# Attention and two MLPs on one core: fp32 scores from q and k turned by TensorE, W1o loaded into buffers of its own, and another loop order in one product

## The chip, the cores and the metric

The kernel runs on one core of a Trainium2 chip. The metric is the device time of one execution in microseconds (us). Engines: PE is TensorE, DVE is VectorE, ACT is ScalarE, POOL is GpSimd, SP is SyncE, which here only issues DMAs. Each engine works through its own instructions in the order in which they are written.

## What is computed

Attention with rotary positions over 4 batches, 8 heads, 576 positions and 64 dimensions; its output, 2304 tokens of 512, goes through two MLPs, 512 to 2048 to 512 each.

```python
q_rot, k_rot = rotate(q), rotate(k)          # x1*cos - x2*sin, x1*sin + x2*cos
scores = (1 / sqrt(D)) * q_rot @ k_rot.T
attn = exp(scores - scores.max(-1)); attn = attn / (attn.sum(-1) + 1e-9)
x = (attn @ v)                               # B, H, S, D -> tokens x 512
h = x @ moe_w_in;  x = (h * sigmoid(1.702 * h)) @ moe_w_out
h = x @ moe2_w_in; out = where(h > 0, h, exp(min(h, 0)) - 1) @ moe2_w_out
```

All tensors are fp32.

## The kernel before

**Numbers.** Nearly every product runs in f16: an operand is scaled by a power of two and split into a high half and a low half, and a product is the sum of three (high x high, high x low, low x high; `THIRD`). Splitting costs one instruction for the high half (ACT or DVE) and one for the low half (DVE) for each tile.

**Order.** A class `Plan` takes operations with their inputs, buffers and a key (constants in `TUNE`) and writes each engine's order out before anything runs. Buffers of a name are few (`BUFS`): two score tiles `s` in PSUM, three general PSUM tiles `m`, two tiles `E` of exponentials. A change of keys or buffers writes all engines' orders anew.

**Attention.** `prep(b, hp)` prepares q and k of one batch and a pair of heads (16 in all): largest magnitude (ACT, L600), its way across the partitions by PE and DVE (L350, L354, L357, L360), the scale (L606 to L612), the rotation (DVE, L618, L622, L626), high halves (ACT, L632, L638), low halves (DVE, L641) and one DMA transpose into `qkT` (L653). `s_unit` is one head against 128 query positions: four f16 products of 288 columns into a score tile `s` (L753), the maximum (DVE, L757) and its product with the scale (L761), the exponential with its sum (ACT, L765), reciprocal (L772, L776), high and low halves (L781, L783, L787) and a DMA transpose into `et` (L796). The last 64 positions of both heads make a "tail" unit of eight products. `av_unit` multiplies with v (L822, L825, L829).

**First MLP.** Tokens go in blocks: 128, 256 and 192 in batch 0, 320 and 256 in the others. `first_mlp` makes first products with W1i (L872; 12 for each of 16 slices), a tanh form of the activation (ACT L875, DVE L878), the halves of g in `ghl` (L887, L890), and second products with W1o (L909), evicted at L915. The first products of a block are written to wait for the second products of the block before (`prev`). W1i and W1o are loaded raw into four buffers `G`, which are the memory of `ghl`: so all W1i loads stand on SP's queue ahead of W1o's, and block 0's halves of g wait for the whole of W1o to be read out (`W1o.raw_done`). `class Weight` finds each matrix's scale (L420 to L453) and splits it (ACT L496, DVE L498 and L502; for W1i's first 12 tiles PE makes the low half, L510 and L511).

**Second MLP.** Five blocks of 512 tokens, the last of 256. First products with W2i (L1104), ELU (ACT L1107, DVE L1111, L1115), halves (L1079, L1082, L1087), then the product with W2o. For block 0 that is L1235: for each of four token tiles, 16 slices of 128 rows, three products each, 192 products of 512 columns. The other blocks use seven quarter-size products on sums of operands (L1180); the sums of W2o's quarters are made behind block 0 (`weight_sums`, DVE L977, ACT L994).

The order of block 0's last product:

```python
for tt in range(n // P):            # 4 token tiles
    for c in range(4):              # 4 chunks of 4 slices of W2o
        ...                         # 12 products, L1235, into the tile's "m" bank
```

Of the kernel before, what the change touches and what calls it, by code (L numbers as in the profile page):

```python
# [20 lines left out]
    s=2, av=1, m=3, E=2, Ehl=3, et=2, qkT=3, N16=1, R=1, V=4, T=1, v16=3, x=9, t=3, y=1, R2=3, yhl=1, o=3,  # L21
)
TUNE = dict(
    pe_w1i=12, pe_w1o=0, lsame=218.42826132665004, tab=-77.15647150906182, f_dve=397.65103425170275, f_act=47.97551796307805, f_pool=12.224437399728332,
    w2s=460.6613102590577, w1i2=-22.170419296187163, w1o2=-231.93668493230768, dlat=823.3988909607715, qh=36.14175031675045,
    kt=-88.54498457451459, vam=-5.163260596687561, p0=0, lat=344.9241913205742, slack=1000000000.0, w1i=-77.58934967679743,
    w1i_s=6.138443343881177, w1o=93.92320162730282, w1o_s=0.9525910530680881, prep0_s=2.7543259438533925, nt=5.6622832505119804,
    s_f=40.3256386921686, mx_f=6.7540349396707375, ex_f=7.075547533776429, av_f=14.806376760777082, prep0=18.144612418330304,
    prep=-131.80876126536305, va0=-49.3683499402336, va=-205.2411204142313, vs=0.522839907570051, tiny=5.266502586522658,
    av=-64.29097871435411, ex=-84.71729381432783, mx=0.5562209547683765, s=-2.701464647252074, tr=-84.32125296728447,  # L30
    bits=-53.84333624001694,
# [190 lines left out]
def kernel(  # L222
# [32 lines left out]
    for b in range(B):  # L255
        parts = ([([0], False), ([1, 2], False), ([3], True)], [([0, 1], True), ([2, 3], False)], [([0, 1], False), ([2, 3], True)])[TUNE['p0'] if b == 0 else 1]
# [52 lines left out]
    buf("qkT", ap_, [P, 6, 5 * P], F16, BUFS["qkT"])  # L309
    n16 = ap_.tile([P, 6, 5, P], F16, name="n16")  # L310
    buf("N16", lambda i: n16, None, None, 1)
    buf("R", ap_, [P, 1280], F32, BUFS["R"])
    buf("V", ap_, [P, 640], F32, BUFS["V"])
    buf("T", ap_, [P, 4, 5, D], F32, BUFS["T"])
# [24 lines left out]
    def across(am, n, hM, after, key, add=False, use=()):  # L339
# [3 lines left out]
        if add:  # L343
            def total(e):
                nc.tensor.matmul(take(hM)[:, 256:256 + n], square, am(), start=True, stop=True)
# [15 lines left out]

        o = op({"pe": 300.0}, turn, list(after) + [ready_c], key, need=[("m", hM)], use=use)
        o = op({"dve": 220.0 + 220.0 * (n > 1)}, most, [o], key, use=[hM], port=n > 1)
        return op({"pe": 200.0}, back, [o, lit], key, use=[hM])

    def max_scale(am, name, bufs, after, key, add=False, mul=1.0):
# [10 lines left out]
        o = across(am, 1, hM, after, key, add)  # L377
# [170 lines left out]
    tab = ap_.tile([P, 10, D], F32, name="tab")  # L548
# [5 lines left out]
    am_t = [per.tile([P, 2], F32, name=f"am{i}") for i in range(2)]  # L554
    ghl = per.tile([P, 2, KF, NMAX], F16, name="ghl")
    gh, gl = ghl[:, 0], ghl[:, 1]
    gflat = ghl.rearrange("p t a b -> p (t a b)")
    buf("G", lambda i: (gh, gl)[i // 2].rearrange("p a b -> p (a b)").bitcast(F32)[:, 1024 * (i % 2):1024 * (i % 2) + 1024], None, None, 4)

    def start(e):  # L560
        nc.sync.dma_start(out=eye, in_=tab_d[:, 10:12, :].rearrange("p a d -> p (a d)"))
        nc.sync.dma_start(out=tab, in_=tab_d[:, 0:10, :])

    def light(e):
        nc.gpsimd.memset(n16[:, 4:6, :, D:2 * D], 0.0)
# [11 lines left out]
    csc = {}  # L577
    am_last = {}

    def prep(b, hp):  # L580
        key = first_u[fb[b], hp] - TUNE["prep"] if b else first_u[0, hp] * TUNE["prep0_s"] - TUNE["prep0"]
        h0 = 2 * hp
        st = {}
        hR, hT, hN, hX, hG = [(x, b, hp) for x in ("R", "T", "N16", "qkT", "qkg")]

        def R5():
            return take(hR).rearrange("p (t h j d) -> p t h j d", t=2, h=2, j=5)

        def load(e):
            R = R5()  # L590
            nc.gpsimd.memset(take(hR).rearrange("p (a f) -> p a f", a=4)[64:P, :, 256:320], 0.0)
            for t, src in enumerate((q, k)):
                nc.sync.dma_start(out=R[:, t, :, 0:4, :], in_=src[b, h0:h0 + 2, 0:512, :].rearrange("h (p j) d -> p h j d", j=4))
                nc.sync.dma_start(out=R[0:64, t, :, 4, :], in_=src[b, h0:h0 + 2, 512:S, :].rearrange("h p d -> p h d"))

        def amax(e):
            am = am_t[hp % 2]
            if e == "act":
                for t in range(2):
# [733 lines left out]
```

## Time and profile before

| | us |
|---|---|
| device time, median of 3 runs | 1068.86 (1068.05 to 1069.65) |
| span of the profiled execution | 1067.2 |
| PE busy | 956.5 (90%) |
| DVE busy | 910.9 (85%) |
| ACT busy | 664.0 (62%) |

The span runs from the first to the last instruction of one profiled execution on the core. A table of stretches gives each engine's busy time, the granted clock of PE and the share of the DMA engines for a part of the span; a timeline gives one engine's instructions with start and duration, neighbours of one kind joined (x12 is twelve instructions), and in brackets the idle time ahead of them with what ended it. Since neighbouring products overlap in the pipeline, a price is read from one row's start to the next one's.

### The profile page before, as it was taken

To read this page: it belongs to the slowest core of one execution; us is meant where nothing else is said; L and a number is where in the kernel's file an instruction comes from. 1 tells how busy PE (TensorE), PEld (TensorE's weight loads), DVE (VectorE), ACT (ScalarE), POOL (GpSimd) and SP (SyncE) were. 2 spreads that over 40 slices of the span, in tenths; PEclk is the share of its full clock that TensorE was granted. 3 is DMA by queue.
4 is the path that set the end of the run, shared out by engine and by line. 5 is a ranking of instruction groups with operands and counts; after the bars stand their busy time and mean duration, and the time that the engine had idled before them with its cause. 6 is when DMAs were issued, how large, how long until landed. Compare 5 with 4: busy or idle time off the path is not lost. (4 is left out here: it accounts for less than half of the span.)

```text
span 1067.2 us, 20467 instructions
## 1 busy us (share of the span) xinstructions
PE 956.5 (90%) x7710; PEld 682.2 (64%) x7710; DVE 910.9 (85%) x2075; ACT 664.0 (62%) x1233; POOL 6.8 (1%) x25
## 2 busy tenths in 40 slices
PE   1457658999989999999999999996999999999997
PEld 0223437877876678876788778642445855855886
DVE  7899999998989999999895979899969669569474
ACT  5688889785868788787563738565246136146141
POOL 0000000000000000000000000000000000000000
PEclk9987669999999999999999999997999999999999
DMA  8899967597878797877754434600000200200100
GB/s 275 242 219 223 232 147 126 123 166 169 165 156 158 141 199 146 159 141 147 168 113 159 156 109 121 212 22 1 21 20 1 65 15 1 65 15 2 45 16 20
DMA packets 295010, 124.94 MB, mean 117 GB/s; under 512 B 264960, under 2 KB 284032, under 8 KB 294912
## 3 DMA queue, kind: packets, MB, share of 16 engines
q1 hardware_dynamic: 294912, 123.64, 50.4%
q8 instruction: 60, 0.98, 0.4%
q14 instruction: 38, 0.31, 0.1%
HBM read 53.35 MB, written 9.44 MB: 59 GB/s over the span
## 5 line engine op out<-in xcount | busy, mean ns | idle before, releaser
L872 PE MATMUL m<-x,wi 128*128 128x256 f16 (+3 forms) x1728 | 199.4, 273 | 1.2 <-DVE t L878 1.1
L909 PE MATMUL m<-ghl,wo 128*128 128x256 f16 (+3 forms) x1728 | 198.7, 273 | 0.3 <-ACT y L915 0.2
L1104 PE MATMUL m<-yhl,w2i 128*128 128x512 f16 (+1 forms) x960 | 188.3, 358 | 0.5 <-DVE e L1115 0.3
L872 PEld LDWEIGHTS <-wi 128*128 128x128 f16 x1728 | 156.7, 98 | 36.1 <-issue 5.5
L909 PEld LDWEIGHTS <-wo 128*128 128x128 f16 x1728 | 157.4, 98 | 33.7 <-issue 3.3
L1104 PEld LDWEIGHTS <-w2i 128*128 128x128 f16 x960 | 93.9, 98 | 92.9 <-issue 1.0
L765 ACT ACTIVATE E<-s,st,qk_c 128x576 f32<-128x576 f32 x144 | 118.7, 826 | 25.4 <-DVE st L761 13.6
L787 DVE SCALAR_TENSOR_TENSOR Ehl<-E,st,Ehl 128x576 f16<-128x576 f32 x144 | 116.6, 813 | 7.4 <-ACT Ehl L781 7.0
L753 PE MATMUL s<-qkT 128*128 128x288 f16 (+1 forms) x640 | 99.6, 302 | 24.4 <-ACT E L765 24.2
L757 DVE TENSOR_REDUCE st<-s 128x1 f32<-128x576 f32 x144 | 107.0, 751 | 7.7 <-PE s L753 7.2
L781 ACT ACTIVATE Ehl<-E,st 128x576 f16<-128x576 f32 x119 | 91.1, 771 | 30.0 <-DMA et<-Ehl 19.6
L1107 ACT ACTIVATE e<-m,y_c 128x512 f32<-128x512 f32 (+1 forms) x80 | 50.8, 639 | 78.0 <-issue 47.9
L753 PEld LDWEIGHTS <-qkT 128*128 128x128 f16 (+1 forms) x640 | 56.5, 104 | 49.8 <-issue 35.9
L1180 PEld LDWEIGHTS <-g 128*128 128x128 f16 x714 | 70.4, 99 | 9.5 <-issue 0.7
L1200 DVE SCALAR_TENSOR_TENSOR x<-z,eo,x 128x256 f32<-128x256 f32 x49 | 23.4, 482 | 50.3 <-PE z L1180 50.0
L875 ACT ACTIVATE t<-m,hsc 128x320 f32<-128x320 f32 (+3 forms) x96 | 55.2, 575 | 14.5 <-PE m L872 12.8
L822 PE MATMUL av<-et,v 128*64 128x256 f16 (+3 forms) x720 | 54.4, 301 | 9.5 <-DMA et<-Ehl 9.3
L887 ACT ACTIVATE ghl<-t 128x320 f16<-128x320 f32 (+3 forms) x96 | 49.9, 521 | 17.9 <-DVE t L878 17.2
L1180 PE MATMUL z<-wo,g 128*128 128x256 f16 x504 | 58.0, 277 | 0.0
L1235 PE MATMUL m<-w2o,g 128*128 128x512 f16 x192 | 50.0, 413 | 8.5 <-DVE w2o L502 5.9
L878 DVE SCALAR_TENSOR_TENSOR t<-t,m 128x320 f32<-128x320 f32 (+3 forms) x96 | 52.7, 551 | 4.2 <-ACT t L875 3.8
L890 DVE SCALAR_TENSOR_TENSOR ghl<-t,ghl 128x320 f16<-128x320 f32 (+3 forms) x96 | 53.1, 554 | 3.4 <-ACT ghl L887 3.2
(172 smaller groups left out, 1389.4 us busy)
## 6 DMA issues: line engine op xcount, KB each, us to landing
ghl<-in_moe_w_in_dram SPq DMA_DIRECT2D x16, 512.0 KB, 5.1
ghl<-in_moe_w_out_dram SPq DMA_DIRECT2D x16, 512.0 KB, 4.7
R<-in_moe_w_in_dram SPq DMA_DIRECT2D x16, 512.0 KB, 4.2
R<-in_moe_w_out_dram SPq DMA_DIRECT2D x16, 512.0 KB, 3.8
R<-in_q_dram SPq DMA_DIRECT2D x16, 256.0 KB, 2.9
R<-in_k_dram SPq DMA_DIRECT2D x16, 256.0 KB, 3.2
V<-in_v_dram SPq DMA_DIRECT2D x32, 128.0 KB, 3.0
R<-y_d SPq DMA_DIRECT2D x8, 512.0 KB, 3.9
```

The lines of the kernel that those rows point to most:

```text
L753: nc.tensor.matmul(o, X[:, a, t], X[:, 2 + 2 * x + a, cs], start=x == 0, stop=x == 1)
L757: nc.vector.tensor_reduce(out=st["t"][:, 0:1], in_=take(hS)[:, :, 0:NS], axis=AX.XY, op=ALU.max, negate=True)
L765: nc.scalar.activation(out=take(hE).rearrange("p (c f) -> p c f", c=2), in_=take(hS)[:, :, 0:NS], func=AF.Exp, bias=t[:, 1:2], scale=csc[b ...
L781: nc.scalar.activation(out=X16[:, 0:S], in_=take(hE), func=AF.Copy, scale=st["t"][:, 3:4])
L787: nc.vector.scalar_tensor_tensor(out=X16[:, S:2 * S], in0=E, scalar=r, in1=X16[:, 0:S], op0=ALU.mult, op1=ALU.subtract)
L822: nc.tensor.matmul(ps[64 * a:64 * a + 64, 0:N], W[:, j, a, :] if w == 2 else V[:, w, j, a, :], T[:, a, blk, 0:N], start=i == 0, stop=i == ...
L872: nc.tensor.matmul(ps, W1i.lhs(kk, u, wl), x[:, xl, 0:N], start=kk == 0 and i == 0, stop=kk == KD - 1 and i == 2)
L875: nc.scalar.activation(out=flat(ht), in_=flat(hM), func=AF.Tanh, scale=hsc[b][:, 1:2])
L890: nc.vector.scalar_tensor_tensor(out=g_of(gl), in0=t_of(), scalar=DOWN / 2, in1=g_of(gh), op0=ALU.mult, op1=ALU.subtract)
L909: nc.tensor.matmul(ps[:, 0:N], W1o.lhs(f, d, wl), (gh, gl)[xl][:, f, 0:N], start=f == 0 and i == 0, stop=f == KF - 1 and i == 2)
L1104: nc.tensor.matmul(ps[:, 0:n], W2i.lhs(kk, u, wl), Y[:, xl, kk, 0:n], start=kk == 0 and i == 0, stop=kk == KD - 1 and i == 2)
L1180: nc.tensor.matmul(ps, AT[A](p, gi, P * tt), BT[B](p, wl), start=p == 0 and i == 0, stop=p == 7 and i == 2)
```

## The change

**Scores in fp32.** Scales, halves and the DMA transpose of q and k are gone. `prep` now rotates q and k (the factor 1/sqrt(D) stands in the table of cosines for q) into a tile `T` that holds both heads side by side, PE turns it in nine transposes of 128x128 (three groups of three, L595), and ACT moves each group of 384 columns into an fp32 `qkT` (L600). `s_units` is both heads of 128 positions at once: four fp32 products of 288 columns, head 0 on rows 0 to 63 and head 1 on rows 64 to 127, into both `s` tiles (L702). Maximum (L707), exponential (L711), halves (L727, L729, L733) and transposes stay one for each head; sum and reciprocal (L718, L722) serve both. In the tail the two heads take the two halves of the keys in opposite order. There are three `E` and two `T` buffers, two `qkT` instead of three.

**W1o and the first blocks.** Raw W1o loads into two buffers of its own (`Go`), and block 0's halves of g no longer wait for it. Batch 0's blocks are 128, 192 and 256 tokens; first products of blocks 0 and 1 (L821) wait for no second product (L858), and block 1's g stands beside block 0's in `ghl`.

**The last product of block 0** in the second MLP (L1180) runs chunk by chunk, all four token tiles within a chunk, on four PSUM banks `z`.

The keys in `TUNE` are others, so all orders are new.

```diff
@@ BUFS
-    s=2, av=1, m=3, E=2, Ehl=3, et=2, qkT=3, N16=1, R=1, V=4, T=1, v16=3, x=9, t=3, y=1, R2=3, yhl=1, o=3,
+    s=2, av=1, m=3, E=3, Ehl=3, et=2, qkT=2, R=1, V=4, T=2, v16=3, x=9, t=3, y=1, R2=3, yhl=1, o=3,
@@ prep
...
+        def turn(e, g):
+            ps = take(hX + (g,))
+            for s in range(3):
+                nc.tensor.transpose(ps[:, P * s:P * s + P], take(hT)[:, 3 * g + s].rearrange("p h d -> p (h d)"), eye)
+
+        def put(e, g):
+            X, ps = take(hX)[:, 3 * P * g:3 * P * g + 3 * P], take(hX + (g,))[:, 0:3 * P]
...
+                nc.scalar.activation(out=X, in_=ps, func=AF.Copy)
...
-        am = op({"act": 2 * c_act(640, acc=1), "dve": c_dve(1280)}, amax, [ld, am_last.get(hp % 2)], key, use=[hR])
-        rd = am_last[hp % 2] = across(lambda: am_t[hp % 2], 2, hG, [am], key)
-        sc = op({"dve": 560}, scale, [rd], key, use=[hG], port=True)
...
-        kh = op({"act": c_act(1280, ptr=1)}, k_hi, [r3, sc], key, need=[("N16", hN)], use=[hR])
-        qh = op({"act": c_act(640, ptr=1)}, q_hi, [kh], key, use=[hR, hN])
-        kl = op({"dve": c_dve(640, ptr=1)}, k_lo, [kh], key, use=[hR, hN], port=True)
-        ql = op({"dve": c_dve(640, ptr=1)}, q_lo, [qh], key, use=[hR, hN], port=True)
-        t = op({"dma": 5200.0}, 2300.0, tr, [ql, kl], key - TUNE["kt"], need=[("qkT", hX)], use=[hN])
...
@@ s_unit, now s_units
         def mm(e):
-            X, ps = take(hX), take(hS)
+            X = take(hX)
             for c in range(2):
-                cs = slice(c * NS, c * NS + NS)
-                for x in range(2):
-                    for a in range(2) if h is None else [h]:
-                        o, t = (ps[64 * a:64 * a + 64, c, 0:NS], slice(512, S)) if h is None else (ps[:, c, 0:NS], slice(j * P, j * P + P))
-                        nc.tensor.matmul(o, X[:, a, t], X[:, 2 + 2 * x + a, cs], start=x == 0, stop=x == 1)
...
+                for a in range(2):
+                    r = slice(64 * a, 64 * a + 64)
+                    if h is None:
+                        w = (c + a) % 2
+                        o, t = take(hS[0])[r, w, 0:NS], S
+                    else:
+                        w = c
+                        o, t = take(hS[a])[:, c, 0:NS], S + 64 + P * j
+                    nc.tensor.matmul(o, X[r, t:t + (TAIL if h is None else P)], X[r, NS * w:NS * w + NS], start=True, stop=True)
...
@@ first_mlp
-                deps = [x_ready[n, kk] for kk in range(KD)] + W1i.slice_ready(v + w) + [prev]
+                deps = [x_ready[n, kk] for kk in range(KD)] + W1i.slice_ready(v + w) + [before]
...
-            o = op({"act": c_act(W * N)}, hi, [o] + (W1o.raw_done if n == 0 else []), -9e4, use=[ht])
+            o = op({"act": c_act(W * N)}, hi, [o], -9e4, use=[ht])
...
-        prev = first_mlp(n, prev, h_ok, y_ok)
+        prev = first_mlp(n, prev if n > 1 else None, prev, h_ok, y_ok)
@@ second_mlp, last product of block 0
-            for tt in range(n // P):
...
-                for c in range(4):
...
+            for c in range(4):
+                for tt in range(n // P):
...
+                    o = op({"pe": c_mm(512, 12)}, lambda e, tt=tt, c=c: mm(e, tt, c), gr[4 * c:4 * c + 4] + W2o.ready[4 * c:4 * c + 4] + prev_out[-1:], kp + 18 + 4 * c + tt, need=[] if c else [("z", hM)], use=[hM] if c else [])
```

On SP, raw W1o loads stood behind all W1i loads; they now stand among the first of these.

PE's order at a score unit, before, while W1i's low halves are made (`eye`, `am0` and `diag2` belong to the turn of the maxima, `wi` to the weights, `s1` is a score tile):

```order
L350 MATMUL m1_480<-eye_75,am0_80 2x128
L510 MATMUL m0_488<-wi_97,w1i_eye_352 128x512
L511 LDWEIGHTS minus_76
L511 MATMUL m0_488<-wi_97,minus_76 128x512
L360 MATMUL m1_480<-diag2_151,square_78 128x2
L753 LDWEIGHTS qkT0_302
L753 MATMUL s1_498<-qkT0_302 128x288
```

And now, among second products of block 0, nine transposes of one `T` and one unit of two heads:

```order
L595 MATMUL m1_1681<-eye_74,T0_1262 128x128 x3
L595 MATMUL m0_1693<-eye_74,T0_1262 128x128 x3
L595 MATMUL m2_1703<-eye_74,T0_1262 128x128 x3
L702 MATMUL s0_1710<-qkT1_1064 128x288
L702 MATMUL s1_1712<-qkT1_1064 128x288
L702 MATMUL s0_1710<-qkT1_1064 128x288
L702 MATMUL s1_1712<-qkT1_1064 128x288
L858 LDWEIGHTS wo_200
L858 MATMUL m1_1723<-ghl_79,wo_200 128x128
```

The turn of the maxima is gone, the transposes have come, and scores of two heads alternate.

PE's order at the place where block 0's second products begin, before (`x` is the attention's output, `wi` and `wo` the weights, `ghl` the halves of g):

```order
L872 MATMUL m0_1766<-x7_1450,wi_97 128x128
L872 LDWEIGHTS wi_97
L872 MATMUL m0_1766<-x7_1450,wi_97 128x128
L909 LDWEIGHTS wo_396
L909 MATMUL m2_1838<-ghl_82,wo_396 128x128
```

And now, where first products of block 1 (192 columns) stand among second products of block 0:

```order
L858 LDWEIGHTS wo_200
L858 MATMUL m1_1723<-ghl_79,wo_200 128x128
L821 LDWEIGHTS wi_93
L821 MATMUL m0_1739<-x1_648,wi_93 128x192
L821 LDWEIGHTS wi_93
```

First products of block 1 no longer stand behind the second products of block 0.

DVE's order at the end of the sums of W2o's quarters, before (`R20` holds a sum, `e0` is a tile of the next block's ELU, `w2o` the weight):

```order
L977 TENSOR_TENSOR R20_9748<-w2o_7745,R20_9748 128x256
L977 TENSOR_TENSOR R20_9748<-R20_9748,w2o_7745 128x256
L977 TENSOR_TENSOR wo_396<-R20_9748,wo_396 128x1024
L1111 TENSOR_SCALAR e0_9854<-e0_9854 128x512
L1115 SCALAR_TENSOR_TENSOR e0_9854<-m2_9825,y_c_8634,e0_9854 128x512
L1082 SCALAR_TENSOR_TENSOR ghl_82<-e0_9854,y_c_8634,ghl_82 128x256
```

And now at the same place:

```order
L926 TENSOR_TENSOR R20_9195<-w2o_7127,R20_9195 128x256
L926 TENSOR_TENSOR R20_9195<-R20_9195,w2o_7127 128x256
L1060 TENSOR_SCALAR e0_9232<-e0_9232 128x512
L1064 SCALAR_TENSOR_TENSOR e0_9232<-m1_9200,y_c_8016,e0_9232 128x512
L926 TENSOR_TENSOR wo_200<-R20_9195,wo_200 128x1024
L1060 TENSOR_SCALAR e1_9254<-e1_9254 128x512
L1031 SCALAR_TENSOR_TENSOR ghl_79<-e0_9232,y_c_8016,ghl_79 128x256
```

The first ELU of the next block stands one instruction earlier, behind 71 of the 72 rows of sums.

## Rows read from the trace of the kernel before

**Rows 1.** The page, busy time of each engine: us (share of the span) xinstructions.

```profile
PE 956.5 (90%) x7710; PEld 682.2 (64%) x7710; DVE 910.9 (85%) x2075; ACT 664.0 (62%) x1233; POOL 6.8 (1%) x25
```

**Rows 2.** Stretches: bounds, us, busy PE, PEld, DVE, ACT, POOL, clock, DMA share, GB/s.

```profile
0.00:189.00 189.00, 104.51 (x913) 67.75 (x914) 172.85 (x410) 149.34 (x283) 3.75 (x15) 0.83 0.88 209
189.00:570.00 381.00, 371.63 (x3557) 296.30 (x3555) 345.00 (x872) 284.83 (x568) 3.07 (x10) 1.00 0.75 152
...
725.00:750.00 25.00, 16.48 (x44) 4.69 (x42) 24.38 (x43) 11.26 (x17) 0.00 (x0) 0.63 0.00 0
...
785.00:1022.00 237.00, 236.60 (x1611) 156.96 (x1610) 175.85 (x359) 95.05 (x140) 0.00 (x0) 1.00 0.09 25
```

**Rows 3.** PE's timeline, 156 to 191 us: start, duration, operation, [idle before].

```profile
158.67 2.17 PE L872 MATMUL m<-x,wi 128*128 128x128 f16 x36
...
188.53 2.64 PE L909 MATMUL m<-ghl,wo 128*128 128x128 f16 x40
```

**Rows 4.** DVE's timeline, 182 to 187 us.

```profile
185.22 0.75 DVE L502 SCALAR_TENSOR_TENSOR wo<-wo,w1o_s 128x512 f16<-128x512 f32 x1
185.88 0.15 DVE L772 TENSOR_SCALAR st<-st 128x1 f32<-128x1 f32 x1
```

**Rows 5.** DVE's groups by form: count | us in all, mean ns of one | idle before.

```profile
L641 DVE SCALAR_TENSOR_TENSOR n<-R,qk_s,n 128x640 f16<-128x640 f32 x32 | 27.9, 877 | 0.6 <-ACT n L632 0.4
...
L761 DVE TENSOR_TENSOR st<-st,qk_c 128x1 f32<-128x1 f32 x144 | 21.3, 152 | 0.3
```

**Rows 6.** PE's waits, 0 to 205 us: us in all, times, longest us.

```profile
PE s L753 <- ACT E L765: 17.9, 16, 3.1
```

**Rows 7.** PE's timeline, 380 to 400 us.

```profile
382.42 0.66 PE L753 MATMUL s<-qkT 128*128 128x288 f16 x4
382.92 1.79 PE L909 MATMUL m<-ghl,wo 128*128 128x320 f16 x12
...
386.77 0.68 PE L753 MATMUL s<-qkT 128*64 128x288 f16 x8
387.38 1.80 PE L909 MATMUL m<-ghl,wo 128*128 128x320 f16 x12
...
394.83 0.38 PE L350 MATMUL m<-eye,am 128*2 128x128 f32 x2
395.15 1.48 PE L872 MATMUL m<-x,wi 128*128 128x256 f16 x12
396.56 0.38 PE L360 MATMUL m<-diag,square 2*128 2x2 f32 x2
396.87 1.48 PE L872 MATMUL m<-x,wi 128*128 128x256 f16 x12
398.19 0.65 PE L753 MATMUL s<-qkT 128*128 128x288 f16 x4
```

**Rows 8.** PE's timeline, 54 to 56 us.

```profile
54.57 1.02 PE L510 MATMUL m<-wi,w1i_eye 128*128 128x512 f32 x2
55.43 0.38 PE L511 MATMUL m<-wi,minus 128*128 128x512 f16 x1
```

**Rows 9.** PE's waits, 189 to 570 us.

```profile
PE s L753 <- ACT E L765: 6.3, 9, 1.3
```

**Rows 10.** PE's timeline, 718 to 786 us.

```profile
722.95 5.34 PE L1235 MATMUL m<-w2o,g 128*128 128x512 f16 x24
...
739.07 0.58 PE L1235 MATMUL m<-w2o,g 128*128 128x512 f16 x1 [0.86 <-DVE w2o L502]
...
746.91 34.59 PE L1235 MATMUL m<-w2o,g 128*128 128x512 f16 x147 [0.17 <-ACT w2o L496]
781.34 4.91 PE L1104 MATMUL m<-yhl,w2i 128*128 128x512 f16 x22
```

**Rows 11.** DVE's timeline, 770 to 786 us.

```profile
776.21 1.23 DVE L977 TENSOR_TENSOR wo<-R,wo 128x1024 f16<-128x1024 f32 x1 [1.12 <-ACT wo L994]
784.85 0.43 DVE L1111 TENSOR_SCALAR e<-e 128x512 f32<-128x512 f32 x1 [7.41 <-ACT e L1107]
```

More of the change, by code (lines that the diff above doesn't have):

```diff
@@ L582, in prep @@
         h0 = 2 * hp
[L583 to L587, printed above, removed]
+        hR, hT, hX = [(x, b, hp) for x in ("R", "T", "qkT")]
         def load(e):
[L590 to L594, printed above, removed]
@@ new lines, in prep @@
+        r0 = op({"dve": c_dve(576)}, lambda e: rope_swap(e, 0), [ld, begin], key, need=[("T", hT)], use=[hR], port=True)
+        r1 = op({"dve": c_dve(576)}, lambda e: rope_swap(e, 1), [ld, begin, r0], key, use=[hR, hT], port=True)
+        r2 = op({"dve": c_dve(1152)}, rope_cos, [r1], key, use=[hR], port=True)
+        r3 = op({"dve": c_dve(1152)}, rope_add, [r2], key, use=[hR, hT], port=True)
+        out = []
+        t = None
+        for g in range(3):
+            t = op({"pe": 360.0}, lambda e, g=g: turn(e, g), [r3, ready_c, t], key, need=[("m", hX + (g,))] + ([] if g else [("qkT", hX)]), use=[hT] + ([hX] if g else []))
+            out.append(op({"act": c_act(384, True)}, lambda e, g=g: put(e, g), [t], key - TUNE["kt"], use=[hX + (g,), hX]))
@@ L764, in ex, with mx @@
+        def mx(e, a):
+            if not a:
+                st["t"] = tiny(6, "st", 6)
+            nc.vector.tensor_reduce(out=st["t"][:, a:a + 1], in_=take(hS[a])[:, :, 0:NS], axis=AX.XY, op=ALU.max, negate=True)
+        def ex(e, a):
             t = st["t"]
             nc.scalar.activation(
[L766 to L767 removed]
+                out=take(hE[a]).rearrange("p (c f) -> p c f", c=2), in_=take(hS[a])[:, :, 0:NS], func=AF.Exp,
+                bias=t[:, a:a + 1], scale=1.0, accum_out=t[:, 2 + a:3 + a],
@@ L854, in y_scale, with first_mlp @@
         return f
-    def first_mlp(n, prev, h_ok, y_ok):
+    def first_mlp(n, before, prev, h_ok, y_ok):
         b, chunks, tail, n0, N = blocks[n]
+        g0 = blocks[0][4] if n == 1 else 0
         kb = MK + 100 * n
@@ new lines, in mm, with ev, dma @@
+            def mm(e, tt, c):
+                ps, g = take(("o2", kb, tt)), g2_tile()
+                for f in range(4 * c, 4 * c + 4):
+                    for i, (wl, gi) in enumerate(THIRD):
+                        nc.tensor.matmul(ps, g[:, f, 512 * gi + P * tt:512 * gi + P * tt + P], W2o.h[:, f, 512 * wl:512 * wl + 512], start=f == 0 and i == 0, stop=f == KF - 1 and i == 2)
+            for c in range(4):
+                for tt in range(n // P):
+                    hM, ho = ("o2", kb, tt), ("e", kb, "o", tt)
+                    r0 = t0 + P * tt
+                    o = op({"pe": c_mm(512, 12)}, lambda e, tt=tt, c=c: mm(e, tt, c), gr[4 * c:4 * c + 4] + W2o.ready[4 * c:4 * c + 4] + prev_out[-1:], kp + 18 + 4 * c + tt, need=[] if c else [("z", hM)], use=[hM] if c else [])
+                    prev_out.append(o)
+                    if c < 3:
+                        continue
+                    def ev(e, hM=hM, ho=ho, st=st):
+                        nc.scalar.activation(out=take(ho), in_=take(hM), func=AF.Copy, scale=st["eo"])
+                    def dma(e, r0=r0, ho=ho):
+                        store(e, take(ho), r0, 0, DM)
+                    o = op({"act": c_act(512, True, 1)}, ev, [o, oe], -1e5, need=[("e", ho)], use=[hM])
+                    op(*dma_in(P * DM * 4), dma, [o], -1e5, use=[ho])
@@ L1296, in _rope_table @@
     rows = np.arange(128)
-    tab = np.zeros((128, 12, D), np.float32)
-    for j in range(4):
-        tab[:, j] = c[4 * rows + j]
-        tab[:, 5 + j] = s[4 * rows + j]
-    tab[:, 4] = c[512 + rows % 64]
-    tab[:, 9] = s[512 + rows % 64]
-    tab[:, 10:12] = np.eye(128, dtype=np.float32).reshape(128, 2, D)
+    tab = np.zeros((128, 20, D), np.float32)
+    scale = np.float32(1.0 / np.sqrt(D))
+    end = 512 + rows % 64
+    part = np.where(rows < 64, np.float32(1.0), scale)[:, None]
+    for i, t in enumerate((c, s)):
+        for j in range(4):
+            tab[:, 9 * i + j] = t[4 * rows + j]
+            tab[:, 9 * i + 5 + j] = t[4 * rows + j] * scale
+        tab[:, 9 * i + 4] = t[end] * part
+    tab[:, 18:20] = np.eye(128, dtype=np.float32).reshape(128, 2, D)
     return tab
```

214 lines of the change are left out of this document (74 added, 140 removed).

## The prediction

> **What bounds the kernel now.** I read the busy shares first [rows 1]: TensorE (PE) has 956.5 of the 1067.2 us, VectorE (DVE) 910.9, so either can set the end of a stage. The table of stretches [rows 2] tells them apart. Up to 189 us PE works 104.51 of 189 us at a mean granted clock of 0.83 (it alternates between the two levels, 1.2 and 2.4 GHz), while DVE has 172.85: DVE leads. From 189 to 570 us PE has 371.63 of 381 at full clock: what PE must do there is the time. From 725 to 750 us PE works 16.48 of 25 and the clock falls to a mean of 0.63; DVE has 24.38. From 785 us PE is full again (236.60 of 237). So a change of PE's work counts from 189 to 570 us, a change of DVE's before that, and PE's waits count around 725 to 785 us.
>
> The place that parts startup from the full stretch is seen on PE's timeline [rows 3]: first products of block 0 from 158.67, with gaps behind them, and second products without a break only from 188.53. The last of W1o's low halves on DVE starts at 185.22 and takes 0.75 [rows 4]; with it all of W1o is ready.
>
> **Startup, to the place where W1o is ready.** On DVE the change takes away the 32 low halves of q and k (27.9 us in all) and 144 products of the maximum with its scale (21.3) [rows 5], makes the rotations 10% narrower, and joins sums and reciprocals of two heads. Counted over the order, with durations of the same forms in this trace and 83 ns less for each (neighbours overlap by about that much: the row at 185.22 lasts 0.75 and the next starts 0.66 later [rows 4]), what stands ahead of W1o's last low half falls from 393 rows and 164.7 us to 325 rows and 160.5: -4 us. Against it stand PE's fp32 scores at half clock: 18 two-head units and 5 tails before the place, whose price (next part) doubles there. PE idles for 84 of the 189 us, so most is hidden, but PE's own waits for scores to be read are 17.9 us already [rows 6], so the loop of scores, maximum and exponential is not slack. I give back 4 us: **0**, with -4 (all hidden) and +12 (18 x about 0.67, none hidden) as bounds. The transposes of q and k leave the DMA engines, 88% busy here [rows 2]; what that brings lies inside the lower bound.
>
> **From 189 to 570 us: PE's work.** Prices from start to next start on PE's timeline [rows 7]: four f16 score products of one head 382.42 to 382.92, 0.50; a tail (two heads in 64 columns each, 8 products) 386.77 to 387.38, 0.61; the turn of the q and k maxima 0.32 and its way back 0.31, 0.63 a pair; twelve first products of 256 columns 396.87 to 398.19, 1.32, or 0.110 each, hence 0.082 for 192 columns.
>
> Not in the trace: fp32 products over 64 rows. An fp32 product of 512 columns appears as two passes, 54.57 to 55.43, 0.43 each [rows 8]; for 288 columns 0.24. A unit of two heads is now four fp32 products, eight passes, the heads in turn on rows 0 to 63 and 64 to 127. One after the other: 8 x 0.24 = 1.92. All pairs side by side: 0.96. In program order a head's second pass waits for its own first, and the other head's first runs beside that second: five steps of 0.24, about 1.20, with a start 1.25. I take 1.25, because tails already run pairs side by side (8 products in 0.61, against 0.125 each alone), and keep 0.96 and 1.92. The same for a tail: 1.0, with 0.8 and 1.92.
>
> Nor does it show fp32 transposes on PE. Nearest is the turn of the maxima, two passes over 128 columns in 0.32 [rows 7], its upper bound; one pass of 128 columns at the fp32 rate is 128/512 x 0.43 = 0.107, its lower. I take 0.12, near the single pass: the turn is two passes and comes alone, the transposes come three in a row.
>
> Behind the place stand, before: 93 one-head units (46.5), 12 tails (7.3), 10 pairs (6.3), and all 192 first products of the block that was 192 wide (16.0; now both first products and that width stand ahead). After: 46 two-head units x 1.25 = 57.5, 11 tails x 1.0 = 11, 99 transposes x 0.12 = 11.9. Small pieces (12 second products of 128 columns +0.7; 28 fewer products with v, two side by side, -1.1) make -0.4. Sum 57.5 + 11 + 11.9 - 46.5 - 7.3 - 6.3 - 16.0 - 0.4 = **+3.9 us**. So the fp32 scores alone cost PE time, and the first products that move ahead into PE's idle time pay most of it.
>
> Of PE's 9.4 idle us in this stretch, 6.3 is waiting for an exponential to free a score buffer, 9 times [rows 9]. A third buffer of exponentials eases that; a unit that needs both score buffers at once makes it harder. I take half, **-3**, bounds -6 and +6.
>
> **The last product of the first token block.** Now it runs token tile by token tile, so the first tile needs all of W2o: after 24 products (722.95) it goes in steps of one to three until 746.91, and ends at 781.34 [rows 10]. With chunks of W2o outside and four banks of their own, 48 products are ready for each chunk: 192 products x 0.217 (147 took from 746.91 to 781.34 with the slow clock at first; 24 took 5.34 less the overlap) = 41.6 from 722.95, that is 764.5, 16.8 earlier; the third chunk's last part comes at 739.07 and the fourth's at 746.91 [rows 10], needed at 743.8 and 754.1. But the next block's ELU stands on DVE behind 71 of the 72 rows of weight sums, the last of which starts at 776.21; DVE then idles 7.41 us until 784.85 [rows 11]. PE, 16.8 earlier, fills three m banks (7.8 us) and waits from 772.3 to about 777.5. What it keeps lies between 7.41 + 1.12 = 8.5 (all work waits on DVE) and 16.8. I take **-10**. Where the clock stays high, nothing else falls late: PE leads from 785 us on.
>
> Sum: span 1067.2 + 0 + 3.9 - 3 - 10 = 1058.1. The profiled execution's span is 1.66 below the median shown (1068.86), taken for what lies around it: **1060 us**.
>
> **What hides what.** Raw W1o in its own two buffers lets it load among W1i's transfers; that no longer waits for block 0's g, and g no longer for it. I cost it at nothing: the end of the stage is DVE's queue, 91% busy. ScalarE loses maxima and high halves of q and k and gains 48 evictions of 384; at 62% [rows 1] it costs nothing unless a unit waits on it.
>
> The Trainium skill (TensorE: Matmul & The Clock Gate, Part 3: Packing small matmuls) says products in different row groups run concurrently, starting within 4 ns. No run here shows it for rows; columns agree (the tail's 0.61). By it a unit could be 0.96, 13 us less over 46 units. [...]
>
> **Rivals.**
> - *Row halves do not overlap* (slower). Place: every score unit behind 189 us, where PE is the bound. Price 1.92 instead of 1.25: 46 x 0.67 = 31, 11 tails x 0.92 = 10; 1060 + 41 = 1101. The balance is lost once a unit costs 0.2 us more than taken, about 1.45 (9 us over 46). For it: no row of this trace has a product over 64 rows. Against: the column pairs.
> - *Row halves overlap wholly*: 0.96, 46 x 0.29 = 13 less: 1047. For it, the tails' pairs; against, order of passes within a head.
> - *Startup grows*: fp32 units at half clock delay maxima and exponentials, W1o is ready some 12 us later: 1072. For it, 17.9 us of such waits now.
> - *Transposes are dear*: 0.28 to 0.32 each, 99 of them, 16 to 20 more: 1076 to 1080. For it, the turn's 0.32.
> - *The chunk order does nothing* (the change does not do what it says): weight sums hold DVE so long that the first block's end moves and the next block's start does not: no -10, 1070. For it, the sums end at 777.4; against, the 7.41 us of idle DVE behind them.
>
> **How the numbers follow.** Chances: forecast 0.49 (its own range 1051 to 1068, from the bounds of the -3 and -10 and of startup), row halves apart 0.14, wholly together 0.16, startup 0.10, dear transposes 0.06, chunk order in vain 0.05. A measurement can tell about 0.2% here, so "same" is 1066.7 to 1071.0. Faster: 0.45 of the forecast and 0.16, 0.61. Same: 0.03 of the forecast and 0.05, 0.08. Slower: 0.01 + 0.14 + 0.10 + 0.06 = 0.31. The range 1042 to 1090 leaves out most of the first rival (0.11) and some 0.08 of the others.
>
> **What would show it.** In the changed kernel: score units from start to next start (1.25 at full clock; 0.96 or 1.92 by the rivals); transposes, three in about 0.36; first products of both early blocks ahead of the first second product, and PE without gaps from about 189 us; the last product of the first block about 42 us long without steps, full clock through it; DVE's last weight sum just ahead of the next block's ELU. I am wrong if a unit costs over 1.45, if PE is full only from 200 us on, or if DVE idles as long behind the sums as before.

## The result, and the profile after

The changed kernel takes 1058.19 us (median of 4, 1057.37 to 1058.97) against 1068.45 for the kernel before beside it: a ratio of 0.990, 95% interval 0.9884 to 0.9917. The forecast was 1060. The profiled span is 1056.4 us, 10.8 less than before.

The engines' busy time on the page, which answers to [rows 1]: PE has more to do, and a larger share of a shorter span.

```profile
PE 978.3 (93%) x7790; PEld 686.8 (65%) x7790; DVE 858.2 (81%) x1688; ACT 608.0 (58%) x1167; POOL 1.7 (0%) x8
```

The stretches, which answer to [rows 2] (bounds, us, busy PE, PEld, DVE, ACT, POOL, clock, DMA share, GB/s):

```profile
0.00:189.00 189.00, 130.06 (x1191) 89.13 (x1192) 167.94 (x334) 141.16 (x285) 1.68 (x8) 0.93 0.82 191
189.00:570.00 381.00, 374.45 (x3359) 280.01 (x3357) 298.26 (x561) 238.12 (x501) 0.00 (x0) 1.00 0.67 120
...
725.00:750.00 25.00, 25.00 (x118) 11.32 (x117) 24.38 (x43) 11.24 (x17) 0.00 (x0) 1.00 0.00 0
750.00:785.00 35.00, 31.07 (x137) 13.63 (x136) 33.83 (x63) 14.31 (x20) 0.00 (x0) 0.95 0.11 31
```

PE now works 130.06 of the first 189 us instead of 104.51, at a clock of 0.93 instead of 0.83. From 189 to 570 us it is as full as before. From 725 to 750 us it has no gap and full clock, where it had 16.48 us and 0.63; a new gap has come between 750 and 785.

PE's timeline in startup, as [rows 3]: first products of block 0 end at 158, then those of block 1 (192 columns) stand among the first second products, and from 162 us on PE is full up to 200. Six transposes take 0.66 us.

```profile
154.11 4.19 PE L821 MATMUL m<-x,wi 128*128 128x128 f16 x72
...
162.29 0.84 PE L858 MATMUL m<-ghl,wo 128*128 128x128 f16 x12
162.98 2.14 PE L821 MATMUL m<-x,wi 128*128 128x192 f16 x24
...
187.58 3.52 PE L858 MATMUL m<-ghl,wo 128*128 128x128 f16 x60
...
196.57 0.82 PE L595 MATMUL m<-eye,T 128*128 128x128 f32 x6
197.23 0.83 PE L858 MATMUL m<-ghl,wo 128*128 128x128 f16 x12
```

The same in stretches, at full clock:

```profile
150.00:175.00 25.00, 23.75 (x312) 20.19 (x308) 24.89 (x52) 23.43 (x52) 0.00 (x0) 1.00 0.57 105
175.00:189.00 14.00, 14.00 (x182) 12.89 (x181) 14.00 (x27) 13.17 (x29) 0.00 (x0) 1.00 0.46 64
```

W1o's low halves on DVE (count: shortest, median and longest in ns, first and last start): the last starts at 186.7, where [rows 4] had 185.22. So W1o is ready no sooner; what PE does until then is more.

```profile
L495 DVE SCALAR_TENSOR_TENSOR wo<-wo,w1o_s x16: 720/736/743, 150.1 to 186.7; 128x512 f16<-128x512 f32 x16
```

Scores on PE's timeline, as [rows 7]: a tail unit takes 383.62 - 382.50 = 1.12 us, a two-head unit 390.22 - 389.05 = 1.17.

```profile
382.50 1.19 PE L702 MATMUL s<-qkT 64*64 64x288 f32 x8 [0.30 <-ACT E L711]
383.62 2.80 PE L770 MATMUL av<-et,v 128*64 128x320 f16 x20
...
389.05 1.24 PE L702 MATMUL s<-qkT 64*128 64x288 f32 x8
390.22 1.28 PE L770 MATMUL av<-et,v 128*64 128x256 f16 x20
```

What is left of PE's waits from 189 to 570 us for exponentials, as [rows 9] (6.3 before):

```profile
PE s L702 <- ACT E L711: 3.6, 5, 1.4
```

The last product of block 0, as [rows 10]: 41.4 us without a step, then 36 products of the next block, then 3.93 us of waiting for DVE.

```profile
722.99 41.60 PE L1180 MATMUL z<-w2o,g 128*128 128x512 f16 x192
764.43 7.93 PE L1053 MATMUL m<-yhl,w2i 128*128 128x512 f16 x36
776.29 35.49 PE L1053 MATMUL m<-yhl,w2i 128*128 128x512 f16 x156 [3.93 <-DVE e L1064]
811.62 1.47 PE L1129 MATMUL z<-w2o,ghl 128*128 128x256 f16 x12
```

DVE there, as [rows 11]: it no longer idles 7.41 us ahead of the ELU; the weight sums run right up to it.

```profile
775.03 0.42 DVE L1060 TENSOR_SCALAR e<-e 128x512 f32<-128x512 f32 x1
775.49 0.75 DVE L1064 SCALAR_TENSOR_TENSOR e<-m,y_c,e 128x512 f32<-128x512 f32 x1
776.24 1.23 DVE L926 TENSOR_TENSOR wo<-R,wo 128x1024 f16<-128x1024 f32 x1
```

After the wait the clock is near its lower level for 3.7 us (stretches of the same view as above):

```profile
772.30:776.30 4.00, 0.07 (x2) 0.01 (x1) 3.86 (x8) 1.15 (x2) 0.00 (x0) 1.00 0.30 66
776.30:780.00 3.70, 3.70 (x10) 1.34 (x10) 3.63 (x7) 2.18 (x4) 0.00 (x0) 0.54 0.01 2
```

The two traces reach the end of the first MLP's products at the same time: the last of them starts at 678.9 us in both (this is the place meant below by the end of the first MLP). In these two executions the whole gain lies behind it.

### The profile page after: what moved, and what is told of

Its sections match the earlier page's. It is cut to its first block, busy times and chain, and to the rows that moved or that the text cites. A ratio compares the mean times of both kernels' runs of the same rounds, so it can differ in the third digit from the quotient of the medians.

```text
span 1056.4 us, 20058 instructions
## 1 busy us (share of the span) xinstructions
PE 978.3 (93%) x7790; PEld 686.8 (65%) x7790; DVE 858.2 (81%) x1688; ACT 608.0 (58%) x1167; POOL 1.7 (0%) x8
## 5 line engine op out<-in xcount | busy, mean ns | idle before, releaser
L821 PE MATMUL m<-x,wi 128*128 128x256 f16 (+3 forms) x1728 | 198.0, 273 | 0.5 <-DVE t L827 0.5
L858 PE MATMUL m<-ghl,wo 128*128 128x256 f16 (+3 forms) x1728 | 197.5, 273 | 0.0
L858 PEld LDWEIGHTS <-wo 128*128 128x128 f16 x1728 | 155.9, 98 | 41.5 <-issue 12.4
L821 PEld LDWEIGHTS <-wi 128*128 128x128 f16 x1728 | 155.7, 98 | 41.8 <-issue 12.5
L733 DVE SCALAR_TENSOR_TENSOR Ehl<-E,st,Ehl 128x576 f16<-128x576 f32 x144 | 116.3, 811 | 26.7 <-ACT Ehl L727 25.7
L711 ACT ACTIVATE E<-s,st 128x576 f32<-128x576 f32 x144 | 106.1, 738 | 49.3 <-DVE st L707 28.9
L702 PE MATMUL s<-qkT 64*128 64x288 f32 (+1 forms) x640 | 116.1, 466 | 10.0 <-ACT E L711 9.9
L727 ACT ACTIVATE Ehl<-E,st 128x576 f16<-128x576 f32 x117 | 89.3, 769 | 54.1 <-DMA et<-Ehl 38.3
L707 DVE TENSOR_REDUCE st<-s 128x1 f32<-128x576 f32 x144 | 107.0, 750 | 11.6 <-PE s L702 11.3
L702 PEld LDWEIGHTS s<-qkT 64*128 64x128 f32 (+1 forms) x640 | 60.3, 191 | 42.1 <-ACT E L711 17.2
L824 ACT ACTIVATE t<-m,hsc 128x320 f32<-128x320 f32 (+3 forms) x96 | 55.4, 577 | 25.1 <-PE m L821 23.2
L1064 DVE SCALAR_TENSOR_TENSOR e<-m,y_c,e 128x512 f32<-128x512 f32 (+1 forms) x80 | 55.0, 690 | 0.4
L770 PE MATMUL av<-et,v 128*64 128x256 f16 (+3 forms) x720 | 50.9, 290 | 3.5 <-DMA et<-Ehl 3.5
```

The source lines that it names most:

```text
L702: nc.tensor.matmul(o, X[r, t:t + (TAIL if h is None else P)], X[r, NS * w:NS * w + NS], start=True, stop=True)
L707: nc.vector.tensor_reduce(out=st["t"][:, a:a + 1], in_=take(hS[a])[:, :, 0:NS], axis=AX.XY, op=ALU.max, negate=True)
L711: nc.scalar.activation(out=take(hE[a]).rearrange("p (c f) -> p c f", c=2), in_=take(hS[a])[:, :, 0:NS], func=AF.Exp, bias=t[:, a:a + 1], s ...
L727: nc.scalar.activation(out=X16[:, 0:S], in_=take(hE[a]), func=AF.Copy, scale=r)
L733: nc.vector.scalar_tensor_tensor(out=X16[:, S:2 * S], in0=E, scalar=r, in1=X16[:, 0:S], op0=ALU.mult, op1=ALU.subtract)
L821: nc.tensor.matmul(ps, W1i.lhs(kk, u, wl), x[:, xl, 0:N], start=kk == 0 and i == 0, stop=kk == KD - 1 and i == 2)
```

## The experiments

Each ratio is against runs of the kernel before on the same chip.

**One part alone: the chunk order in the kernel before.** The edit puts the changed kernel's loop over chunks, with its four z banks, into the kernel before:

```diff
-            for tt in range(n // P):
-                ...
-                for c in range(4):
+            for c in range(4):
+                for tt in range(n // P):
```

> The kernel before with one part of the change alone: the last product of the first token block runs chunk by chunk on four z banks. Theory (this part carries the whole gain, since in both traces the first MLP ends at 678.9 us): 11 us less than before, about 1057.5, the product 41.6 us long at full clock, then 4 us of PE waiting behind the weight sums. Rival (it shares the gain with the fp32 scores, whose lighter DVE load lets the weight sums go sooner): 1060 to 1066.

Measured: 1061.29 us, ratio 0.9924 (0.9903 to 0.9945), some 8 us less. The stage itself does what the theory says:

```profile
725.87 41.60 PE L1231 MATMUL z<-w2o,g 128*128 128x512 f16 x192
767.31 7.93 PE L1104 MATMUL m<-yhl,w2i 128*128 128x512 f16 x36
779.18 35.51 PE L1104 MATMUL m<-yhl,w2i 128*128 128x512 f16 x156 [3.93 <-DVE e L1115]
```

Start to start the product takes 767.31 - 725.87 = 41.4 us, then the same wait of 3.93. From the end of the first MLP to the last product, this kernel takes 374.0 us and the kernel before 384.8: 10.8 less. In this profiled execution the first MLP ended 3 us later (681.8) than in that of the kernel before, though PE's order up to there is the same: startup differs that much between two executions. It would account for a ratio smaller than the stage's gain, but one trace does not show that.

**That part undone in the changed kernel.**

> The changed kernel with that one part undone: the last product of the first block runs token tile by token tile again. Theory: 1069, the time of before, since everything up to 679 us costs the same in both. Rival: under 1066, if the other parts bring something that the chunk order now hides.

Measured: 1068.19 us, ratio 0.998 (0.9962 to 0.9999). The steps are back, and the product ends at 781.46, as before:

```profile
781.46 8.80 PE L1053 MATMUL m<-yhl,w2i 128*128 128x512 f16 x40
```

Its first MLP ends at 679.2. Both runs say the same: the chunk order carries the gain, and all other parts together bring 0 to 4 us by the interval, 0 by the traces. The traces tell this to within 2 or 3 us only: in the changed kernel, this one and the three runs on the weight sums below, whose PE order is the same up to there, the first MLP ends between 677.3 and 679.2.

**The order of heads in a unit.**

```diff
-            for c in range(2):
-                for a in range(2):
+            for i in range(4):
+                c, a = (i // 2, i % 2) if h is None else (i % 2, i // 2)
```

> The changed kernel, in which the four fp32 products of a two-head unit run head 0 first (both column halves), then head 1, instead of in turn; tails as they are. Tells what the two records are that start 7 ns apart in each of a unit's four steps. If these are the two heads on the two halves of the rows: only the seam between the heads overlaps, seven steps of 0.24 and 0.2 for the changes of shape, 1.85 instead of 1.17 a unit; 46 units behind 189 us make +31, and some of the 18 before it, so 1085 to 1100. If these are the two passes of one product: 1.17 as before, 1058.

Measured: 1056.89 us, ratio 0.9882 (0.9862 to 0.9902), no different from the changed kernel, and a unit takes 1.18:

```profile
393.24 1.25 PE L702 MATMUL s<-qkT 64*128 64x288 f32 x8
394.42 5.41 PE L821 MATMUL m<-x,wi 128*128 128x256 f16 x48
```

From this alone the second reading (two passes of one product) looked right. The next run refutes it.

**Both heads on the same rows.** In full units `r` is rows 0 to 63 for both heads, so head 1's own scores are not computed.

> The changed kernel, in which both heads' products of a two-head unit read rows 0 to 63, so that head 1 gets the scores of head 0 (a part of the computation is wrong that way; tails as they are). Head order changed nothing, so the pair of records 7 ns apart is not two heads. If it is the two passes of one 64-row product, which fit wherever its rows are: 1.17 us a unit, 1058. If two products share the array only from different halves: 2.1 us a unit, 46 x 0.96 = 44 more, 1100.

Measured: 1105.21 us, ratio 1.0326 (1.0305 to 1.0346), and 2.14 us a unit:

```profile
384.82 2.20 PE L703 MATMUL s<-qkT 64*128 64x288 f32 x8
386.96 1.28 PE L771 MATMUL av<-et,v 128*64 128x256 f16 x20
```

So the pair is two products on different halves of the rows. In whichever order the heads are written, PE works through the two halves' products side by side: in the head-first kernel too the trace's records start in pairs, 13 ns apart (7 in turn), so head 1's first pass runs ahead of head 0's second, which is written earlier. Here PE does not keep to the written order, which I had put down as a rule for every engine. On the same rows the eight passes go one by one, 0.242 apart in the records, with 0.10 more at either end (the first and the last step last 0.33 to 0.35).

**Every score product twice.**

```diff
-            for c in range(2):
-                for a in range(2):
+            for i in range(8):
+                c, a = i // 2 % 2, i % 2
```

> The changed kernel with every score product issued twice, in the same place of all orders; the outputs stay. Measures whether a microsecond of PE behind 189 us is one of the time, on which the sum and the slower rival rested. Theory: a two-head unit has eight steps of 0.24 instead of four, 0.96 more; 46 units and 11 tails behind 189 us make +55, the 23 ahead of it add up to 22 where PE is idle for a third of the time: 1113 to 1130. Rival (waits for exponentials or DMA take the place of PE's work): under 1095.

Measured: 1117.24 us, ratio 1.043 (1.0399 to 1.046), as forecast; a unit 2.14:

```profile
387.67 2.21 PE L702 MATMUL s<-qkT 64*128 64x288 f32 x16
389.81 1.28 PE L770 MATMUL av<-et,v 128*64 128x256 f16 x20
```

The first MLP ends at 733.0, 54 later, and 46 units x 0.97 with 11 tails x 0.97 are 55. (The profiled execution is the fastest of the four, 1111.75.) That the two agree so closely is partly chance: from 189 us on PE's work grows by 60, since some 5 us of other work fall behind that place too, and its idle time falls from 7.0 to 0.9 us. So behind 189 us a microsecond of PE is nearly one of time, and the waits that are left there take up a few.

**Block 1's first products wait again.**

```diff
-        prev = first_mlp(n, prev if n > 1 else None, prev, h_ok, y_ok)
+        prev = first_mlp(n, prev, prev, h_ok, y_ok)
```

> The changed kernel with one wait put back: first products of block 1 wait for the second products of block 0. Raw W1o keeps its own buffers. Theory (W1o is ready on DVE at 187 us, and what PE does ahead of that is free): the 192 first products of 192 columns, 16 us of PE's work, fall behind the place, 10 to 16 us more than the changed kernel, 1068 to 1074. Rival (the order matters little because scores fill PE's idle time instead): under 1062.

Measured: 1081.41 us, ratio 1.0105 (1.0088 to 1.0122), some 22 us more than the changed kernel and beyond the forecast. In startup PE idles again and its clock falls (stretches), with more than twice the changed kernel's 7.3 us of waiting for exponentials (waits, 0 to 205 us):

```profile
150.00:175.00 25.00, 17.89 (x237) 14.19 (x234) 24.90 (x50) 21.51 (x47) 0.00 (x0) 0.97 0.53 103
175.00:189.00 14.00, 9.79 (x65) 6.65 (x65) 13.15 (x23) 11.56 (x25) 0.00 (x0) 0.70 0.79 158
189.00:200.00 11.00, 10.34 (x130) 8.71 (x131) 10.16 (x18) 6.61 (x15) 0.00 (x0) 0.84 0.83 123
```

```profile
PE s L702 <- ACT E L711: 15.8, 7, 5.5
```

The first MLP ends at 700.8, 21.9 later. By the sum of starts to next starts over PE's records from 189 us on, first products take 181.8 us instead of 165.4 there (+16.4), and idle time is 9.2 instead of 7.0; the rest, some 3 us, is second products and scores, some of them at the lower clock that follows the gaps (0.84 from 189 to 200 us), which I had left out.

**The whole W1o part undone.**

```diff
-    W1o = Weight(..., "w1o", "Go", ...)
+    W1o = Weight(..., "w1o", "G", ...)
-            o = op({"act": c_act(W * N)}, hi, [o], -9e4, use=[ht])
+            o = op({"act": c_act(W * N)}, hi, [o] + (W1o.raw_done if n == 0 else []), -9e4, use=[ht])
-        prev = first_mlp(n, prev if n > 1 else None, prev, h_ok, y_ok)
+        prev = first_mlp(n, prev, prev, h_ok, y_ok)
```

> The changed kernel with the whole W1o part undone: raw W1o goes through the memory of ghl behind W1i, block 0's halves of g wait until all of it is read out, and block 1's first products wait for block 0's second ones. What stays is fp32 scores and the chunk order. Theory: as with the wait alone or later, 1068 to 1080, since buffers of its own were costed at nothing and W1o is DVE's work. Rival (the load order held the startup): 1085 or more.

Measured: 1081.47 us, ratio 1.0101 (1.0077 to 1.0126): a little beyond the forecast's upper end, and the same as with the wait alone. The order is another one: W1o's low halves end by 149 us, but first products start only at 170.7, and PE goes through its work from 150 to 175 us at near the lower clock (0.59).

```profile
L495 DVE SCALAR_TENSOR_TENSOR wo<-wo,w1o_s x16: 732/744/752, 108.6 to 147.8; 128x512 f16<-128x512 f32 x16
```

```profile
150.00:175.00 25.00, 21.24 (x152) 15.11 (x153) 19.58 (x38) 13.44 (x32) 0.00 (x0) 0.59 0.59 110
```

So in net buffers of its own bring W1o nothing here without the first products that PE makes ahead, as costed. The two orders differ throughout, and that the two times agree to 0.1 us is chance.

**f16 scores with the other two parts.** The kernel before with `Go`, the three blocks, the first products ahead and the chunk order (two `qkT`, two tanh tiles).

> The kernel before (f16 scores, q and k turned by DMA) with the other two parts of the change: raw W1o in two buffers of its own, blocks of 128, 192 and 256 tokens with the first products of two blocks ahead, and the chunk order. For room it has two qkT instead of three and two tanh tiles instead of three; its keys are those of the kernel before. Theory (behind 189 us the fp32 scores cost PE some 17 us, which the first products ahead pay): faster than the changed kernel, 1036 to 1048. Rival (in startup DVE has the low halves of q and k and the products of maxima as well, so W1o is ready later and PE's idle time there is lost anyway): 1055 to 1065.

Measured: 1082.72 us, ratio 1.0099 (1.0074 to 1.0124): both readings missed it. W1o's last low half starts at 225.9 us, 39 later than in the changed kernel:

```profile
L502 DVE SCALAR_TENSOR_TENSOR wo<-wo,w1o_s x16: 733/742/752, 189.5 to 225.9; 128x512 f16<-128x512 f32 x16
```

Behind that place PE's work to the end of the first MLP is 459.7 us, 23 less than the changed kernel's behind 189 us (482.8): the theory's half on PE's work holds. With the later place the first MLP ends at 690.1, 11 us later. The other 15 of the 26 us by which the span is longer are lost behind it, in the second MLP: W2o's first high half starts at 740.8 us on ACT instead of 711.1, PE waits 6.8 us for the largest magnitude of W2o from DVE, and 5.1 for the next block's ELU. The keys are those of the kernel before, and its order has W1o's last low half at DVE's row 459 instead of 393. So I moved that key:

> The kernel e7_f16_Go with one key changed (that of W1o, 93.9 to 75), which puts W1o's last low half at row 406 of DVE's order instead of 459 (it was 393 in the kernel before and is 325 in the changed kernel). Tells whether e7 was late because its orders put W1o late, or because f16 scores leave no room for the early products. Theory (what counts is the place where W1o is ready and the PE work behind it): ready near 195 us instead of 226, 20 to 30 us less than e7, 1050 to 1062. Rival (DVE's and PE's work of q and k in f16 fills the startup anyway): 1070 or more.

Measured: 1086.08 us, ratio 1.0142 (1.0111 to 1.0173). W1o's last low half starts at 209.3, 16.6 us sooner, and the time is no better:

```profile
L502 DVE SCALAR_TENSOR_TENSOR wo<-wo,w1o_s x16: 733/744/752, 168.5 to 209.3; 128x512 f16<-128x512 f32 x16
```

First products now start at 175.9, not at 169.7, and the first MLP ends at 697.7, 7.5 us later than with the other key. Yet both kernels start the second block's products with W2i at 787.7: in both the last product of block 0 waits for W2o, whose first high half starts at 740.5 here and at 740.8 there. So the place of W1o does not set the time of these two runs, and they do not tell what f16 scores cost or bring. Whether f16 scores with the early products could be faster under other orders stays open.

**The weight sums.** First their order: the planner is told 2.24, 1.72 and 1.24 us for the three steps of a sum, near what they take in the trace.

> The changed kernel, in which the planner is told longer times for the weight sums on DVE, so that the first ELU of the second token block stands behind 58 of the 72 rows of sums instead of 71. Theory (PE's 3.9 us of waiting at 772 to 776 and the half clock that follows it are lost to the sums): 5.5 us less than the changed kernel, about 1052.7, full clock through 765 to 811. Rival (the sums come as much later, and the products that use them wait, near 820 us): 1056 to 1058.

Measured: 1055.26 us, ratio 0.9874 (0.9849 to 0.9899); the interval overlaps the changed kernel's, so a gain of 3 us is not shown. The one wait of 3.9 us has become several (PE's waits behind 764 us), while DVE is as full as ever:

```profile
PE m L1053 <- DVE e L1064: 2.2, 3, 1.4
...
PE z L1129 <- DVE wo L926: 1.0, 1, 1.0
```

```profile
772.00:780.00 8.00, 7.44 (x36) 3.28 (x34) 7.97 (x16) 4.46 (x7) 0.00 (x0) 1.00 0.00 0
780.00:790.00 10.00, 8.58 (x44) 4.10 (x43) 9.86 (x20) 5.73 (x9) 0.00 (x0) 1.00 0.01 2
```

So another order of the sums does not free PE there, and DVE's work may be what holds it (7.97 of 8 us and 9.86 of 10 busy). What the trace gained is 0.6 us of waiting, and the 1.7 us that the lower clock behind the one long wait had cost; 1.6 of the 3.4 us by which its span is shorter lie ahead, where the first MLP ends at 677.3. The test of DVE's work is to take some of it off:

```diff
+            pool = f in (3, 6)
+            eng = nc.gpsimd if pool else nc.vector
```

> The changed kernel, in which POOL, which is idle there, makes two of the eight groups of weight sums (slices 3 and 6), some 8 us less for DVE between 730 and 811 us. Theory, new since DVE's order alone gave back less than PE's wait (DVE is busy from 725 to 811 us, so its work there sets the time): PE's 3.9 us at 772 us go, 4 to 6 us less than the changed kernel, 1052 to 1054. Rival (POOL is slow or shares a port with DVE, whose instructions get longer): 1058 or more.

Measured: 1059.13 us, ratio 0.9883 (0.9865 to 0.9901), no gain over the changed kernel. The same sums in the changed kernel and then in this one (count | us, mean ns of one | idle before):

```profile
L926 DVE TENSOR_TENSOR e<-w2o 128x512 f32<-128x512 f16 x16 | 11.0, 688 | 0.3
...
L926 DVE TENSOR_TENSOR R<-e 128x256 f32<-128x256 f32 x16 | 6.8, 425 | 0.6
```

```profile
L929 DVE TENSOR_TENSOR e<-w2o 128x512 f32<-128x512 f16 x12 | 10.0, 836 | 0.2
...
L929 POOL TENSOR_TENSOR e<-w2o 128x512 f32<-128x512 f16 x4 | 7.8, 1957 | 687.3 <-DVE g L1074 675.3 <-DVE R L929 11.8
...
L929 DVE TENSOR_TENSOR R<-e 128x256 f32<-128x256 f32 x12 | 7.0, 587 | 0.4
```

The means of DVE's own sums grow from 688 to 836 ns and from 425 to 587, and POOL needs 1957 for what DVE does in 688. What POOL takes over, DVE loses beside it: its sums take 41.2 us in all, where the changed kernel's eight groups took 41.0. So the last run makes DVE's work less without another engine:

```diff
+                if f in (3, 6):
+                    nc.vector.memset(take(hs), 0.0)
+                    return
```

> The changed kernel, in which DVE fills two of the eight groups of weight sums (slices 3 and 6) with zeros instead of making them (a part of the computation is left out that way); all orders stay, POOL does nothing. Some 2.7 us less for DVE for each group, 5.4 in all. Theory (DVE's work sets the time from 725 to 811 us): PE's 3.9 us at 772 us and the half clock behind them go, its next products start about 5 us sooner, 1052.5 to 1054. Rival (only the order holds PE, or a later wait takes its place): 1056.5 to 1059.

Measured: 1053.73 us, ratio 0.9841 (0.9818 to 0.9863). The long wait is gone, and the next products with W2o start at 806.76 instead of 811.62, 4.9 us sooner, for the 5.2 us of work that DVE no longer has (two fillings of 0.91 and two subtractions of 0.42 in place of 7.8):

```profile
764.47 18.29 PE L1059 MATMUL m<-yhl,w2i 128*128 128x512 f16 x84
783.21 23.72 PE L1059 MATMUL m<-yhl,w2i 128*128 128x512 f16 x108 [0.45 <-DVE e L1070]
806.76 1.47 PE L1135 MATMUL z<-w2o,ghl 128*128 128x256 f16 x12
```

So DVE's work from 725 us on sets when PE can go on behind the last product, to 811 us. Some 1.2 us of the gain are lost again further on: the span is 3.6 less.

## Why the prediction was right

The sum was 0 + 3.9 - 3 - 10, and the time came out 2 us under the 1060. Step by step, with PE's records from 189 us to the end of the first MLP, each from its start to the next start, idle time set apart (both kernels are counted from 189 us, so the first line is not added again):

| term, us | forecast | measured |
|---|---|---|
| place where W1o is ready | 0 | +1.5 (185.22 to 186.7) |
| f16 scores and tails gone | -53.8 | -55.4 |
| fp32 units and tails (46, 11) | +68.5 | +68.3 |
| transposes (99) | +11.9 | +11.7 |
| turns of maxima and their way back | -6.3 | -7.0 |
| first products moved ahead | -16.0 | -15.5 |
| small pieces | -0.4 | +0.7 |
| PE's work behind 189 us | +3.9 | +2.8 |
| PE's waits there | -3 | -2.8 (9.85 to 7.04) |
| last product and what follows | -10 | -11 |

**Startup.** The net of 0 was right by its result, and only one of its two halves came as forecast. Up to the end of W1o's last low half DVE works 3.6 us less (169.96 to 166.39), where I had 4. DVE's idle time there grows by 5.0, which gives back the rest; but I had put that on PE's waits for exponentials, and those fall from 17.9 to 7.3 us. DVE waits longer for several things instead, for scores 2.9 us (1.5 before) and for raw W1i 7.2 (6.2 before). My bound of +12 took 0.67 us a unit without working it out; by its own prices at half clock, 2.5 against 2.0, it is 0.5. In place of the forecast's idle PE there is work: from 162 us on PE does the first products of block 1, and its clock does not fall (1.00 from 150 to 189 us). The rival of a longer startup, 12 us, did not come.

**The unit's price** was right in size and wrong in mechanism. I took 1.25 from half overlap, a head's second pass waiting in program order while the other head runs beside it. The runs show whole overlap at 0.24 a step, four steps, and 0.10 at either end, where neighbours use all 128 rows: 4 x 0.242 + 0.2 = 1.17. So the rival of whole overlap had the mechanism, and its 0.96 left out the ends. The Trainium skill (TensorEngine Tiling (Array Packing), Key Properties) says that a change of the tiling mode drains TensorE; the 0.10 at either end of each unit agrees. The change of number type does not cost it: transposes in fp32 on all 128 rows, between f16 products, take 0.66 for six and nothing more. That the line of the table agrees so well (+68.5, +68.3) is partly luck: 46 x 1.17 and 11 tails x 1.12 make 66.1, and the other 2 us come almost all from three units whose heads did not start together. The slower rival's price was too low: with the halves' overlap taken away a unit takes 2.14, not 1.92, and the kernel 1105 with the units alone, where I had 1101 with tails.

**Transposes** take 0.11 each in a row of six (0.66 in all from 196.57 to 197.23): the lower bound was the answer. No run shows the rival's 0.28 to 0.32.

**The last product.** The product itself ends 16.9 us earlier (781.34 to 764.43), as worked out. PE waited 3.93 us where I had about 5, then lost 1.7 to the lower clock (0.54 for 3.7 us), which I had not counted; the next block's products with W2o start 11.2 us earlier. That the gain is cut by the weight sums is right, and as the last run shows it is their work on DVE that cuts it, not only their place.

**What the net hides.** Fp32 scores cost PE 17.6 us behind 189 us (68.3 + 11.7 - 55.4 - 7.0), and the first products ahead pay 15.5 of it and more: without them the kernel is 22 us slower. By PE's work the change is two large moves against each other and one gain that stands apart.

## What to carry to other kernels

Split a span into the stretches that different engines set, price each part of a change only in the stretch where it counts, and look for work that can move into the idle time of the engine that is full later: here 16 us of first products paid for dearer scores. A reduction over weights that are still arriving goes with the weights' chunks outside and as many accumulators as there are output tiles; a gapless PE keeps its clock as well. When a wait ends with another engine's long queue, see whether that engine is full around it: reordering a full engine moves the wait and does not remove it.

## What the runs showed of the hardware

- Products on rows 0 to 63 and on rows 64 to 127 run side by side whatever order they are written in: 1.17 us a unit with heads in turn, 1.18 head by head, 2.14 on the same rows. The Trainium skill (TensorE: Matmul & The Clock Gate, Part 3: Packing small matmuls) says that row groups run concurrently with starts some 4 ns apart; the trace has 7 ns in turn and 13 ns head by head.
- A stretch of 64-row products among 128-row ones costs 0.10 us going in and 0.10 coming out, the same for four steps (1.17) and for eight (2.14).
- An fp32 transpose of 128x128 takes PE 0.11 us in a row of several, one pass of 128 columns at half the f16 rate (an f16 product of 128 columns takes 0.056 there).
- DVE's tensor_tensor slows from 425 to 587 ns and from 688 to 836 on average when POOL does the same work beside it for part of the time.
